# First-group transposes regrouped, chunk loads halved and one weight load moved, at the start of a six-layer cross-network kernel

## The chip, the cores and the metric

The kernel runs on one core of a Trainium2 chip. Times are device microseconds (us). "Time" is a whole execution; "span" is the profiled one, from its first to its last instruction, and is about 1.8 us shorter. PE is the matmul engine (TensorE), DVE is VectorE, ACT is ScalarE; SP is the engine whose queue issues nearly all transfers (DMA).

## The reference

```python
B, F, D, L = 16384, 26, 16, 6        # Din = F*D = 416
x = x0                               # [B, Din] bf16
for l in range(L):
    proj = jnp.einsum('bd,de->be', x, ws[l]) + bs[l]
    x = x0 * proj + x
return x
```

The features number 416 = 3 x 128 + 32. The last 32, the "tails", are handled apart. The kernel keeps the features on the partitions, so x0 must be turned (transposed) on its way in.

## The kernel before

The rows are cut into 8 groups of 2048, a group into 4 chunks of 512. Groups 1 to 7 are turned by the DMA. Group 0 has no time for that: its chunks are loaded as they lie, PE turns them by a matmul with the identity, and ACT and DVE copy the result out of PSUM. The work items are pairs of group and layer, (g, l), in a wavefront order: (0,0), then (1,0), then (0,1), and so on. A pair has three "tiles" of 128 output features, and tails.

Instructions are added one by one with the data that they read and write; a solver derives the semaphore waits. Each engine and each DMA queue keeps the order in which its instructions were added. A transfer on the SP queue that must wait holds up every transfer added after it.

```python
def load_group(g, between=lambda: None):
    ...
    turn(0)                                            # DMA transposes of x0, to SBUF
    add("sp", lambda h: h.dma_start_transpose(Tb, x0[rows, D - P:D]), ...)   # the tails, turned
    turn(1)
    turn(2)
    between()
    for j in range(NJ):                                # four copies: tails to their quadrants
        add("sp", ... h.dma_start(x0s[s][q, XW:XW + CH], Tb[P - T32:P, j * CH:(j + 1) * CH]) ...)
    if turn_of(g, 1):                                  # rotation: waits for the four copies to land
        rotate(x0s[s][:, XW:XW + CH], x0s[s][:, XW + CH:XW + 2 * CH], turn_of(g, 1), ...)
# ... cut: order of the first transfers on SP
load_nat(0, 0, 2)
load_nat(0, 2, KK)
load_wm(0, "sp")                                       # first weights, layer 0
for j in range(1, NJ):
    load_nat(j, 0, KK)                                 # chunks 1 to 3 of group 0
load_w3(0, "sp")
load_group(1, lambda: load_wm(1, "sp"))                # second weights: ahead of the tails' copies
load_wm(2, "sp")
load_w3(2, "sp")

def transposed_chunk(j):
    ba, bb = ((0, 1), (3, 0), (1, 3), (0, 1))[j]       # PSUM banks
    first = (0, P, 2 * P, D - P)                       # 4 x 128 columns: the last holds 32 new ones
    ...                                                # 16 transposes, 2 copies on ACT, 2 on DVE

def first_job():                                       # pair (0, 0)
    transposed_chunk(0)
    ...                                                # bias
    keep_busy(8, 3)                                    # filler matmuls, to hold PE's clock
    full(g, l, 0, ba, True, True, chunks=[0])
    full(g, l, 1, bb, True, True, chunks=[0])
    transposed_chunk(1)
    transposed_chunk(2)
    full(g, l, 0, ba, True, True, chunks=[1])
    transposed_chunk(3)
    load_w3(1, "act")
    full(g, l, 1, bb, True, True, chunks=[1])
    full(g, l, 0, ba, True, True, chunks=[2, 3])
    rows32(g, l, 0, ba, False)                         # the first 32-row matmuls
    ...
```

Of the kernel before, what the change touches and what calls it, by code (L numbers as in the profile page):

```python
# [3 lines left out]
P = 128  # L4
CH = 512
T32 = 32

ACT_F = mybir.ActivationFunctionType
# [13 lines left out]
class Program:  # L22
# [12 lines left out]
    def add(self, eng, fn, reads=(), writes=(), lane=None, batch=None, hold=False, release=False):  # L35
        op = Op(eng, fn, lane, batch)
        deps = {}
        if eng == "pool":
            writes = list(writes) + ["pool"]
        for t in reads:  # L40
            w = self.writer.get(t)
            if w is not None:
                deps[id(w)] = (w, True)
        for t in writes:
            w = self.writer.get(t)
            if w is not None:
                deps[id(w)] = (w, True)
            for r in self.readers.get(t, ()):
                if id(r) not in deps:
                    deps[id(r)] = (r, False)  # L50
        for d, raw in deps.values():
            if d.lane is None and d.eng == eng and lane is None and (eng == "pe" or not raw):
                continue
            op.deps.append(d)
        for t in reads:
            self.readers.setdefault(t, []).append(op)
        for t in writes:
            self.writer[t] = op
            self.readers[t] = []
        if eng == "dve":  # L60
            if hold:
                self.flush()
                self.held = op
            else:
                self.queue[eng].append(op)
                if release:
                    self.flush()
        else:
            self.queue[eng].append(op)
        if lane is not None:  # L70
            batches = self.lanes.setdefault(lane, [])
            if not batches or batches[-1][0] != batch:
                batches.append((batch, []))
            batches[-1][1].append(op)
        return op
# [123 lines left out]
def bass_standalone__cross_network_dcn__recsys_kernel(  # L199
# [6 lines left out]
    B, D = x0.shape  # L206
# [46 lines left out]
    def cols(t, j):  # L253
        return slice(t * GC + j * CH, t * GC + (j + 1) * CH)

    def x0_tok(s, t, j):
        return ("x0", s, t, j)
# [7 lines left out]
    def slot(g):  # L265
        return g % NX0
# [12 lines left out]
    def load_wm(l, eng):  # L279
        add(eng, lambda h: h.dma_start(wm[l][:, :, :], ws[l, 0:NT * P, :].rearrange("(t p) f -> p t f", p=P)),  # L280
            writes=[("wm", l)], lane=f"wm{l}", batch=0)

    def load_w3(l, eng):
        for j in range(NJ):
            add(eng, lambda h, j=j: h.dma_start(w3[l][j * T32:(j + 1) * T32, :], ws[l, NT * P:D, :]),
                writes=[("w3", l, j)], lane=f"w3{l}", batch=0)

    def load_group(g, between=lambda: None):
        s = slot(g)
        rows = slice(g * GC, (g + 1) * GC)  # L290
        def turn(t):
            add("sp", lambda h: h.dma_start_transpose(
                x0s[s][:, t * GC:(t + 1) * GC], x0[rows, t * P:(t + 1) * P]),
                writes=[x0_tok(s, t, j) for j in range(NJ)], lane=f"x0_{s}_{t}", batch=g)

        turn(0)
        add("sp", lambda h: h.dma_start_transpose(Tb, x0[rows, D - P:D]),
            writes=[("ost", t, j) for t in range(NT + 1) for j in range(NJ)], lane="Tb", batch=g)
        turn(1)
        turn(2)  # L300
        between()
        for j in range(NJ):
            q = slice(j * T32, (j + 1) * T32)
            add("sp", lambda h, q=q, j=j: h.dma_start(x0s[s][q, XW:XW + CH], Tb[P - T32:P, j * CH:(j + 1) * CH]),
                reads=[("ost", 0, 0)], writes=[("x03q", s, j)], lane=f"x03_{s}", batch=g)

        if turn_of(g, 1):
            rotate(x0s[s][:, XW:XW + CH], x0s[s][:, XW + CH:XW + 2 * CH], turn_of(g, 1),
                   x03_toks(s), ("x03r", s), f"x03r_{s}", g)

    def x03_toks(s):
        return [("x03q", s, j) for j in range(NJ)]
# [207 lines left out]
    def load_nat(j, k0, k1):  # L520
        add("sp", lambda h: h.dma_start(x0n[:, j, k0:k1, :], perm(g0, j)[:, k0:k1, :]),  # L521
            writes=[("nat", j, k) for k in range(k0, k1)], lane=f"nat{j}{k0}", batch=0)
# [6 lines left out]
    load_nat(0, 2, KK)  # L529
    load_wm(0, "sp")  # L530
    for j in range(1, NJ):
        load_nat(j, 0, KK)
    load_w3(0, "sp")
    load_group(1, lambda: load_wm(1, "sp"))
    load_wm(2, "sp")
    load_w3(2, "sp")

    def keep_busy(n, b):

        for _ in range(n):  # L540
            add("pe", lambda h: h.matmul(bank(b, n=P), ones[:, :], ones[:, :], start=True, stop=True),
                reads=["ones"], writes=[("ps", b)])
# [3 lines left out]
    def psum_t(b):  # L546
        return psum[:, b * CH:(b + 1) * CH].bitcast(BF16)

    def transposed_chunk(j):
        ba, bb = ((0, 1), (3, 0), (1, 3), (0, 1))[j]  # L550
        s = slot(0)
        first = (0, P, 2 * P, D - P)
        seq = [(t, k) for t in range(NT) for k in range(KK)]
        if j == 0:
            seq = [(t, k) for k2 in (0, 2) for t in range(NT) for k in (k2, k2 + 1)]
        for n, (t, k) in enumerate(seq + [(NT, k) for k in range(KK)]):
            if j == 0 and n == NT * 2:
                keep_busy(2, 3)
            b, o = (ba, t * CH) if t < 2 else (bb, (t - 2) * CH)
            c = slice(o + k * P, o + (k + 1) * P)  # L560
            add("pe", lambda h, t=t, k=k, b=b, c=c: h.transpose(  # L561
                psum_t(b)[:, c], x0n[:, j, k, first[t]:first[t] + P], ident[:, :]),
                reads=[("nat", j, k), x0_tok(nat, 0, 0), "ident"], writes=[("ps", b)])
        for t in range(2):
            add("act", lambda h, t=t: h.activation(  # L565
                x0s[s][:, cols(t, j)], psum_t(ba)[:, t * CH:(t + 1) * CH], ACT_F.Copy),
                reads=[("ps", ba)], writes=[x0_tok(s, t, j)])
        add("dve", lambda h: h.tensor_copy(x0s[s][:, cols(2, j)], psum_t(bb)[:, 0:CH]),  # L568
            reads=[("ps", bb)], writes=[x0_tok(s, 2, j)])
        q = slice(j * T32, (j + 1) * T32)  # L570
        add("dve", lambda h: h.tensor_copy(x0s[s][q, XW:XW + CH], psum_t(bb)[P - T32:P, CH:2 * CH]),
            reads=[("ps", bb)], writes=[("x03q", s, j)])

    def first_job():

        g, l = 0, 0
        start_job(g, l)
        transposed_chunk(0)
        bt = 7
        for t in range(NT):  # L580
            add("pe", lambda h, t=t: h.transpose(
                psum_t(bt)[:, t * 8:t * 8 + L], brow[0:L, t * P:(t + 1) * P], ident[0:L, 0:L]),
                reads=["brow", "ident"], writes=[("ps", bt)])
        for j in range(NJ):
            q = slice(j * T32, (j + 1) * T32)
            add("pe", lambda h, j=j, q=q: h.matmul(
                psum_t(bt)[q, NT * 8:NT * 8 + L], brow[0:L, NT * P:D], ident[0:L, 0:L],
                is_transpose=True, tile_position=(0, j * T32)),
                reads=["brow", "ident"], writes=[("ps", bt)])
        add("act", lambda h: h.activation(  # L590
            bias[:, :, :], psum_t(bt)[:, 0:32].rearrange("p (t l) -> p t l", l=8)[:, :, 0:L], ACT_F.Copy),
            reads=[("ps", bt)], writes=["bias"])
        keep_busy(8, 3)
        ba, bb = [4, 5, 6, 7], [2, 3, 0, 1]
        full(g, l, 0, ba, True, True, chunks=[0])
        full(g, l, 1, bb, True, True, chunks=[0])
        transposed_chunk(1)
        transposed_chunk(2)
        full(g, l, 0, ba, True, True, chunks=[1])
        transposed_chunk(3)  # L600
        load_w3(1, "act")
        full(g, l, 1, bb, True, True, chunks=[1])
        full(g, l, 0, ba, True, True, chunks=[2, 3])
        rows32(g, l, 0, ba, False)
        evacuate(g, l, 0, ba, [0, 1], 2, vector=[2, 3])
        full(g, l, 1, bb, True, True, chunks=[2, 3])
        rows32(g, l, 1, bb, False)
        rows32(g, l, 2, ba, True)
        evacuate(g, l, 1, bb, list(range(NJ)), 2)
        full(g, l, 2, ba, False, True, lambda j: evacuate(g, l, 2, ba, [j], 1))  # L610
        finish_tile(g, l, NT)
        tails([(g, l)])
# [341 lines left out]
```

## Time and profile before

| | before |
|---|---|
| time, median of 3 runs | 476.69 us (476.66 to 477.77) |
| span of the profiled run | 475.7 us |
| PE busy | 462.2 us, 97% |
| PE's share of the chain of waits | 95% |

The page of the kernel before: busy time by engine, then the chain that ended last, by engine.

```profile
PE 462.2 (97%) x3325; PEld 195.7 (41%) x3379; DVE 404.0 (85%) x696; ACT 342.4 (72%) x372; POOL 6.8 (1%) x15
...
PE 95%; issue 1%; DMA 1%; ACT 1%; DVE 1%; SPq 0%
```

PE is the limit nearly everywhere. The timeline of PE (columns: start, length, engine, line, operation, count; in brackets the idle time before and what ended it) shows where the start is not dense.

```profile
4.01 0.72 PE L561 MATMUL ps<-ident,x 128*128 128x128 bf16 x10
...
5.81 1.24 PE L456 MATMUL ps<-x,wm 128*128 128x512 bf16 x5 [0.25 <-ACT x L565]
7.92 1.07 PE L561 MATMUL ps<-ident,x 128*128 128x128 bf16 x16 [0.87 <-DMA x<-in_x_dram]
9.56 1.05 PE L561 MATMUL ps<-ident,x 128*128 128x128 bf16 x16 [0.57 <-DVE x L568]
10.45 0.81 PE L456 MATMUL ps<-x,wm 128*128 128x512 bf16 x3
11.10 1.06 PE L561 MATMUL ps<-ident,x 128*128 128x128 bf16 x16
12.21 1.89 PE L456 MATMUL ps<-x,wm 128*128 128x512 bf16 x8
14.03 0.40 PE L477 MATMUL ps<-x,w 32*128 32x512 bf16 x4
...
22.78 0.61 PE L477 MATMUL ps<-x,w 32*128 32x512 bf16 x8
23.32 5.35 PE L456 MATMUL ps<-x,wm 128*128 128x512 bf16 x24
28.60 0.43 PE L471 MATMUL ps<-x,w 32*32 32x512 bf16 x16
```

L561 are the transposes, L456 the 128-row matmuls, L477 the 32-row ones. At 7.92 and 9.56 us PE resumes after waiting for the second and the third chunk. (The view names a DVE copy at 9.56; the landing records show that chunk complete at 9.42.) From there it has no wait. The piece at 23.32 us holds 24 matmuls: the second tile of pair (1,0), then, from the 13th matmul at 25.92 us on, the first tile of pair (0,1). That is the first user of the second weights.

The SP queue in the same stretch (here the length is the time that the queue spent on the issue).

```profile
13.60 4.38 SPq L292 DMA_TRANSPOSE x<-in_x_dram  x2
18.02 0.59 SPq L280 DMA_DIRECT2D wm<-in_ws_dram  x1
18.66 2.52 SPq L304 DMA_DIRECT2D x<-ost  x4
22.55 0.53 SPq L325 DMA_DIRECT2D x<-x  x1
23.12 0.60 SPq L326 DMA_DIRECT2D x<-x  x1
23.76 0.58 SPq L280 DMA_DIRECT2D wm<-in_ws_dram  x1
```

The second weights (L280 at 18.02) landed at 21.82 us, 4 us before their use. L304 are the four copies of the tails; L325 and L326, the rotation, sit waiting from 21.2 to 22.55 us for those copies to land; only then can the third weights (L280 at 23.76) be issued. They landed at 26.90 us, 3.1 us later.

### The profile page before, as it was taken

To read this page: it belongs to the slowest core of one execution; us is meant where nothing else is said; L and a number is where in the kernel's file an instruction comes from. 1 tells how busy PE (TensorE), PEld (TensorE's weight loads), DVE (VectorE), ACT (ScalarE), POOL (GpSimd) and SP (SyncE) were. 2 spreads that over 40 slices of the span, in tenths; PEclk is the share of its full clock that TensorE was granted. 3 is DMA by queue.
4 is the path that set the end of the run, shared out by engine and by line. 5 is a ranking of instruction groups with operands and counts; after the bars stand their busy time and mean duration, and the time that the engine had idled before them with its cause. 6 is when DMAs were issued, how large, how long until landed. Compare 5 with 4: busy or idle time off the path is not lost.

```text
span 475.7 us, 8355 instructions
## 1 busy us (share of the span) xinstructions
PE 462.2 (97%) x3325; PEld 195.7 (41%) x3379; DVE 404.0 (85%) x696; ACT 342.4 (72%) x372; POOL 6.8 (1%) x15
## 2 busy tenths in 40 slices
PE   7999999999999999999999999999999999999995
PEld 6344444444444444444444444434444444444442
DVE  2888888888888888898889869988888888888896
ACT  4677777777777777777777777777777777777785
POOL 1000000000000000000000000000000000000000
PEclk9999999999999999999999999999999999999999
DMA  8866950640002397369308940990000039025899
GB/s 223 181 150 137 190 113 1 142 81 1 28 7 44 63 228 158 76 139 244 84 21 195 208 108 9 178 279 2 1 10 25 4 64 242 15 45 117 227 155 288
DMA packets 138363, 53.31 MB, mean 112 GB/s; under 512 B 112330, under 2 KB 137428, under 8 KB 138324
## 3 DMA queue, kind: packets, MB, share of 16 engines
q1 hardware_dynamic: 137848, 52.46, 49.2%
q8 instruction: 26, 0.43, 0.4%
q10 hardware_dynamic: 476, 0.32, 0.2%
q14 instruction: 13, 0.11, 0.1%
HBM read 5.97 MB, written 13.63 MB: 41 GB/s over the span
## 4 chain that ended last, share of the span: by engine, by line
PE 95%; issue 1%; DMA 1%; ACT 1%; DVE 1%; SPq 0%
PE ps L456 77%; PE ps L477 7%; PE ps L497 6%; PE ps L798 2%; DMA x<-in_x_dram 1%; PE ps L471 1%; ACT tw L394 1%; PE ps L561 1%; PE ps L488 1%; DVE x L864 0%; PE ps L809 0%; ACT x L852 0%; DVE x L858 0%; PE ps L841 0%; SPq L521 0%
## 5 line engine op out<-in xcount | busy, mean ns | idle before, releaser
L394 ACT ACTIVATE tw<-ps,bias 128x1024 bf16<-128x1024 f32 (+1 forms) x295 | 299.8, 1071 | 119.8 <-PE ps L477 80.7
L456 PE MATMUL ps<-x,wm 128*128 128x512 bf16 x1638 | 371.7, 379 | 5.8 <-issue 3.7
L456 PEld LDWEIGHTS ps<-x,wm 128*128 128x128 bf16 x1692 | 158.9, 98 | 213.5 <-issue 27.9
L403 DVE TENSOR_TENSOR tw<-tw,x 128x1024 bf16<-128x1024 bf16 (+1 forms) x285 | 192.3, 682 | 52.8 <-ACT tw L394 52.4
L408 DVE TENSOR_TENSOR x<-tw,x 128x1024 bf16<-128x1024 bf16 (+1 forms) x285 | 183.0, 682 | 0.0
L477 PE MATMUL ps<-x,w 32*128 32x512 bf16 x512 | 39.2, 379 | 0.0
L497 PE MATMUL ps<-x,wm 128*32 128x512 bf16 x564 | 33.0, 380 | 0.0
L434 ACT ACTIVATE ts<-ps,bias 128x512 bf16<-128x512 f32 x47 | 28.8, 701 | 0.0
L438 DVE TENSOR_TENSOR x<-ts,x 128x512 bf16<-128x512 bf16 x47 | 18.6, 417 | 3.7 <-DMA x<-x 3.6
L497 PEld LDWEIGHTS ps<-x,wm 128*32 128x32 bf16 x564 | 13.8, 96 | 17.6 <-issue 5.3
L477 PEld LDWEIGHTS ps<-x,w 32*128 32x128 bf16 x512 | 7.8, 92 | 27.6 <-issue 27.1
L436 DVE TENSOR_TENSOR ts<-ts,x 128x512 bf16<-128x512 bf16 x47 | 18.5, 417 | 0.0
L666 POOL COPY ost<-ot 128x512 bf16<-128x512 bf16 x6 | 5.4, 898 | 423.7 <-DMA ot<-x 423.7
L798 PE MATMUL ps<-wm,x 128*128 128x416 bf16 x48 | 9.5, 340 | 0.0
L852 ACT ACTIVATE x<-ps 128x416 bf16<-128x416 f32 x16 | 7.7, 533 | 2.0 <-PE ps L798 1.9
L568 DVE COPY x<-ps 128x512 bf16<-128x512 bf16 x4 | 1.7, 424 | 8.7 <-PE ps L561 8.7
L565 ACT ACTIVATE x<-ps 128x512 bf16<-128x512 bf16 x8 | 4.3, 594 | 5.6 <-PE ps L561 5.6
L798 PEld LDWEIGHTS ps<-wm,x 128*128 128x128 bf16 x48 | 4.3, 98 | 4.2 <-issue 1.0
L561 PE MATMUL ps<-ident,x 128*128 128x128 bf16 x64 | 4.6, 226 | 1.4 <-DMA x<-in_x_dram 0.9
L858 DVE TENSOR_TENSOR x<-x,x 128x832 bf16<-128x832 bf16 (+1 forms) x10 | 5.0, 504 | 1.1 <-ACT x L852 1.1
L488 PE MATMUL ps<-x,w 32*32 32x512 bf16 x188 | 5.9, 374 | 0.0
L471 PE MATMUL ps<-x,w 32*32 32x512 bf16 x208 | 5.6, 385 | 0.0
(38 smaller groups left out, 35.7 us busy)
## 6 DMA issues: line engine op xcount, KB each, us to landing
out_dram<-ost SPq DMA_DIRECT2D x6, 1664.0 KB, 7.1
x<-in_x_dram SPq DMA_DIRECT2D x7, 416.0 KB, 8.0
x<-x SPq DMA_DIRECT2D x24, 96.0 KB, 2.2
wm<-in_ws_dram SPq DMA_DIRECT2D x6, 312.0 KB, 3.7
out_dram<-ost SPq DMA_DIRECT2D x2, 832.0 KB, 6.7
x<-x SPq DMA_DIRECT2D x22, 64.0 KB, 2.0
out_dram<-x SPq DMA_DIRECT2D x3, 416.0 KB, 3.6
x<-ost SPq DMA_DIRECT2D x28, 32.0 KB, 2.2
```

What stands on the lines that cost most here:

```text
L394: add("act", lambda h, a=a, w=w, b0=b0: h.activation(tw[r][:, a * CH:(a + w) * CH], psum[:, b0 * CH:(b0 + w) * CH], ACT_F.Identity, bias=b ...
L403: add("dve", lambda h, a=a, e=e: h.tensor_tensor(tw[r][:, a * CH:e * CH], tw[r][:, a * CH:e * CH], x0s[s0][:, i * GC + a * CH:i * GC + e * ...
L408: add("dve", lambda h, a=a, e=e: h.tensor_tensor(xs[so][:, i * GC + a * CH:i * GC + e * CH], tw[r][:, a * CH:e * CH], src(i, a, e), ALU.ad ...
L434: add("act", lambda h: h.activation(ts[r][:, :], bank(b), ACT_F.Identity, bias=bias[:, 3, l:l + 1], scale=1.0), reads=[("ps", b), "bias"], ...
L436: add("dve", lambda h: h.tensor_tensor(ts[r][:, :], ts[r][:, :], x03, ALU.mult), reads=[("ts", r)] + tok0, writes=[("ts", r)], release=True)
L438: add("dve", lambda h: h.tensor_tensor(x3s[so][:, :], ts[r][:, :], res, ALU.add), reads=[("ts", r)] + rtok, writes=[("x3", so), ("x3", so, ...
L456: add("pe", lambda h, t=t, j=j: h.matmul(bank(banks[j]), wm[l][:, t, ecols], src(t, j, j + 1), start=(first and t == 0), stop=(not first a ...
L471: add("pe", lambda h, q=q, j=j, r=r, c=c, o=o: h.matmul(psum[o, banks[j] * CH:(banks[j] + 1) * CH], w3[l][q, i * P + c * T32:i * P + (c + ...
L477: add("pe", lambda h, q=q, j=j, r=r: h.matmul(bank(banks[j]), w3[l][q, ecols], src[q, :], start=first, stop=not first, tile_position=(r * ...
L488: add("pe", lambda h, l=l, b=b, s3=s3, ri=ri, qi=qi, ro=ro, qo=qo: h.matmul(psum[qo, b * CH:(b + 1) * CH], w3[l][qi, NT * P:D], s3[qi, :], ...
L497: add("pe", lambda h, t=t, j=j, src=src, l=l, b=b, ro=ro, qo=qo: h.matmul(psum[qo, b * CH:(b + 1) * CH], wm[l][:, t, NT * P:D], src(t, j, ...
L798: add("pe", lambda h, t=t: h.matmul(bank(b, n=D), xcol(t, j, kk), wm[l][:, t, :], start=(first and t == 0), stop=(not first and t == NT - 1)),
```

## The change

The intent, as I read it from the edit: fewer transposes (the tails of all four chunks at once on the four column tiles of the array, in place of a fourth 128-column transpose for each chunk), less waiting for loads and banks, and tails of group 1 that come earlier, since PE is to need them earlier.

```diff
-        load_nat(j, 0, KK)
+        load_nat(j, 0, 2)
+        load_nat(j, 2, KK)
...
-    load_group(1, lambda: load_wm(1, "sp"))
+    load_group(1)
+    load_wm(1, "sp")
...
 def transposed_chunk(j):
-        ba, bb = ((0, 1), (3, 0), (1, 3), (0, 1))[j]
+        ba, bb = ((0, 1), (3, 0), (6, 7), (0, 1))[j]
...  # 12 transposes, first row half then second; copies: 2 on ACT, 1 on DVE
+    def transposed_tails(b):
+        for k in range(KK):
+            for j in range(NJ):
+                o = slice(j * T32, (j + 1) * T32)
+                add("pe", lambda h, j=j, k=k, o=o: h.matmul(
+                    psum_t(b)[o, k * P:(k + 1) * P], x0n[:, j, k, NT * P:D], ident[:, :],
+                    is_transpose=True, tile_position=(0, j * T32)), ...)
+        add("dve", lambda h: h.tensor_copy(x0s[s][:, XW:XW + CH], psum_t(b)[:, 0:CH]), ...)
...
-        keep_busy(8, 3)
+        keep_busy(5, 3)
...
         full(g, l, 0, ba, True, True, chunks=[1])
+        full(g, l, 1, bb, True, True, chunks=[1])
         transposed_chunk(3)
+        transposed_tails(7)
         load_w3(1, "act")
-        full(g, l, 1, bb, True, True, chunks=[1])
         full(g, l, 0, ba, True, True, chunks=[2, 3])
```

## The prediction

> **What bounds the kernel now.** The page gives TensorE (PE) 462.2 us busy of a 475.7 us span (97%); the chain of waits is 95% PE. From about 12 us on that chain is matmuls and short "issue" steps, with no wait for a transfer. So only the first 26 us, which the change touches, can move the time, and each us won or lost there reaches the end.
>
> The start is gated by the loads of the first group. In the chain the second chunk's load ends at 7.88 us; its 16 transposes take 1.08 us; the third chunk's start at 9.56. The waits view blames a VectorE copy for that gap; the landings show the third chunk at about 9.4, so I read it as the load. Both come late from one of 16 DMA engines, 1.4 to 1.9 us behind the others. From 9.56 to 14.10 PE is full: 32 transposes and 12 matmuls.
>
> **What the change does.**
> 1. Transposes: 64 full ones (about 65 ns each in the timeline) become 48, plus 16 tail transposes on four column tiles. After 9.5 us PE has 18 full ones left instead of 32: about -0.9 us. The tails cost about 0.5 us, an estimate: the Trainium skill, "TensorE: Matmul & The Clock Gate" (Wait — 56ns, not 53.3ns?), gives a floor of about 25 ns start to start, and "TensorEngine Tiling (Array Packing)" (Key Properties) says that a switch of tiling mode drains the array. In this trace 12 column-tile matmuls of 512 columns take 0.76 us, so tiles do overlap; no run yet shows the short ones.
> 2. Halved loads: the first half is turned while the second flies; the second halves land no earlier. Three more issues of about 0.48 us go on the SP queue, mostly hidden, since it is held up there (an input transpose issue takes 4.1 us against about 2.1 later).
> 3. VectorE makes one tail copy of 0.43 us instead of four; own banks remove possible bank waits. Fewer filler matmuls: nothing.
> Sum on PE by 14 us: -0.3 us (0 to -0.6).
> 4. The second weights move behind the next group's tails and their rotation. Before, they were issued at 18.02 and landed at 21.8; PE needs them at 25.97. After, the tails go out 0.6 us earlier and land near 21.8; the rotation copies wait for that and take 1.2 us; the weights are issued at about 23.1. The third weights landed 3.1 us after issue, so these land at 26.2 to 26.8. PE would arrive at about 25.6: a new PE wait of 0.5 to 1.2 us, which swallows the gain.
>
> **Net.** PE enters that tile at about 26.3 instead of 25.97: +0.3 us. Predicted 477.0 us against 476.69, 8 in 10 within 475.6 to 478.4. Faster by over 2%: 0.5%; within 2%: 99%; slower: 0.5%.
>
> **What would show it.** (a) Chunk transposes in bursts of 6, the first before 7.9 us. (b) One burst of 16 tails of about 0.5 us near 12.5 us. (c) Chunks two and three of tile 0 done near 13.8. (d) A PE wait for the second weights' transfer near 25.6 us, up to 1.2 us: the decisive one. (e) From there on the same time to the end.
>
> **What would make it wrong.** The weights land under 3 us from issue: the gain of about 0.3 us survives. The extra issues are not hidden and shift the next group's transposes by up to 1.4 us: the wait grows to 2 us and more. The slow DMA engine is a chance of this run. Column-tile transposes dearer than 60 ns each would eat step 1. The three runs before spread over 1.1 us, more than the effect.

## The result

| | before | changed |
|---|---|---|
| time, median of 6 runs | 477.32 us (476.66 to 477.77) | 477.90 us (477.53 to 479.31) |
| ratio | | 1.0018, 95% interval 1.0003 to 1.0033 |
| span of the profiled run | 475.7 us | 476.2 us |

A ratio is the mean time of one kernel's fast runs over that of the other's fast runs of the same rounds, so it is not quite the ratio of the medians. The change made the kernel longer by a hair, within 2%. The page of the changed kernel:

```profile
PE 468.3 (98%) x3376; PEld 195.3 (41%) x3376; DVE 402.6 (85%) x693; ACT 342.0 (72%) x372; POOL 6.2 (1%) x15
...
PE 93%; SPq 4%; DVE 1%; ACT 1%; DMA 0%; issue 0%
```

The PE busy times do not compare: of the matmuls of before 54 have no record (3325, beside 3379 weight loads), of the changed kernel none. By the weight loads, PE does three matmuls fewer (3376), the three fillers. The new item is SPq, the SP queue, with 4% of the chain. PE's timeline of the changed kernel (L559 transposes, L579 the tail transposes, L455 128-row matmuls, L476 32-row ones, L470 the marker):

```profile
4.16 0.85 PE L559 MATMUL ps<-ident,x 128*128 128x128 bf16 x6
...
5.82 1.45 PE L455 MATMUL ps<-x,wm 128*128 128x512 bf16 x6
7.11 1.50 PE L559 MATMUL ps<-ident,x 128*128 128x128 bf16 x24
8.52 1.74 PE L455 MATMUL ps<-x,wm 128*128 128x512 bf16 x6
10.10 0.83 PE L559 MATMUL ps<-ident,x 128*128 128x128 bf16 x12
10.87 0.41 PE L579 MATMUL ps<-ident,x 128*32 128x128 bf16 x16
11.21 1.50 PE L455 MATMUL ps<-x,wm 128*128 128x512 bf16 x6
12.64 0.40 PE L476 MATMUL ps<-x,w 32*128 32x512 bf16 x4
...
21.83 0.61 PE L476 MATMUL ps<-x,w 32*128 32x512 bf16 x8 [0.16 <-DMA x<-ost]
22.37 2.76 PE L455 MATMUL ps<-x,wm 128*128 128x512 bf16 x12
26.43 2.75 PE L455 MATMUL ps<-x,wm 128*128 128x512 bf16 x12 [1.29 <-DVE x L407]
29.11 0.43 PE L470 MATMUL ps<-x,w 32*32 32x512 bf16 x16
```

PE reached the first 32-row matmuls at 12.64 us instead of 14.03. Nine us later it waits 0.16 us for the tails, and then it stands still from 25.14 to 26.43 us. The marker, which comes right after the first user of the second weights, is at 29.11 us instead of 28.60: 0.5 us late, as the span is. So 1.4 us were won and 1.9 us lost. (From start to start the two stops cost 0.22 and 1.45 us, as the idle time in brackets begins only where the last matmul's end is modelled; the other 0.2 us went at the eight 32-row matmuls near 14.4 us, which took 0.76 us to the next start, before 0.54.) The SP queue of the changed kernel:

```profile
12.78 5.15 SPq L292 DMA_TRANSPOSE x<-in_x_dram  x2
17.97 2.51 SPq L303 DMA_DIRECT2D x<-ost  x4
21.80 0.53 SPq L324 DMA_DIRECT2D x<-x  x1
22.38 0.60 SPq L325 DMA_DIRECT2D x<-x  x1
23.02 1.12 SPq L280 DMA_DIRECT2D wm<-in_ws_dram  x2
```

L324 and L325, the rotation, had to wait until 21.80 us for the tails' copies, and the second weights (the first of the two L280 at 23.02) come after it. Their last piece landed at 26.29 us, and PE goes on at 26.43. The waits view of the changed kernel, between 20 and 30 us, names other causes, DVE for the matmul and ACT for its weight load (columns: who, for whom, total, times, longest):

```profile
PEld ps L455 <- ACT tw L393: 1.8, 1, 1.8
PE ps L455 <- DVE x L407: 1.3, 1, 1.3
PEld ps L476 <- DMA x<-ost: 0.6, 1, 0.6
```

DVE's addition (L407) did end at 26.31 us by its timeline, but by the program it makes output of pair (1,0), which this tile of pair (0,1) does not read. The view takes the release that came last by its records, so the name alone decides nothing. The experiments have to.

### The profile page after: what moved, and what is told of

It is laid out like the page before. It is cut to its first block, busy times and chain, and to the rows that moved or that the text cites. A ratio compares the mean times of both kernels' runs of the same rounds, so it can differ in the third digit from the quotient of the medians.

```text
span 476.2 us, 8401 instructions
## 1 busy us (share of the span) xinstructions
PE 468.3 (98%) x3376; PEld 195.3 (41%) x3376; DVE 402.6 (85%) x693; ACT 342.0 (72%) x372; POOL 6.2 (1%) x15
## 4 chain that ended last, share of the span: by engine, by line
PE 93%; SPq 4%; DVE 1%; ACT 1%; DMA 0%; issue 0%
PE ps L455 76%; PE ps L476 7%; PE ps L496 7%; PE ps L811 2%; SPq L292 2%; PE ps L470 1%; SPq L520 1%; SPq L297 1%; PE ps L487 1%; ACT tw L393 0%; DMA x<-ost 0%; SPq L303 0%; SPq L285 0%; DVE x L877 0%; DVE x L407 0%
## 5 line engine op out<-in xcount | busy, mean ns | idle before, releaser
L455 PE MATMUL ps<-x,wm 128*128 128x512 bf16 x1692 | 379.8, 380 | 1.4 <-DVE x L407 1.3
L455 PEld LDWEIGHTS ps<-x,wm 128*128 128x128 bf16 x1692 | 158.6, 98 | 215.5 <-issue 28.2
L407 DVE TENSOR_TENSOR x<-tw,x 128x1024 bf16<-128x1024 bf16 (+1 forms) x285 | 182.9, 682 | 0.0
L476 PE MATMUL ps<-x,w 32*128 32x512 bf16 x512 | 39.4, 379 | 0.2 <-DMA x<-ost 0.2
L496 PEld LDWEIGHTS ps<-x,wm 128*32 128x32 bf16 x564 | 13.8, 96 | 17.6 <-issue 5.3
L476 PEld LDWEIGHTS ps<-x,w 32*128 32x128 bf16 x512 | 7.8, 92 | 28.1 <-issue 27.1
L470 PE MATMUL ps<-x,w 32*32 32x512 bf16 x208 | 5.6, 385 | 0.0
L877 DVE TENSOR_TENSOR x<-x,x 128x832 bf16<-128x832 bf16 x8 | 4.6, 586 | 0.4 <-DMA x<-x 0.4
```

The costliest lines, as they stand in the source:

```text
L407: add("dve", lambda h, a=a, e=e: h.tensor_tensor(xs[so][:, i * GC + a * CH:i * GC + e * CH], tw[r][:, a * CH:e * CH], src(i, a, e), ALU.ad ...
L455: add("pe", lambda h, t=t, j=j: h.matmul(bank(banks[j]), wm[l][:, t, ecols], src(t, j, j + 1), start=(first and t == 0), stop=(not first a ...
L470: add("pe", lambda h, q=q, j=j, r=r, c=c, o=o: h.matmul(psum[o, banks[j] * CH:(banks[j] + 1) * CH], w3[l][q, i * P + c * T32:i * P + (c + ...
L476: add("pe", lambda h, q=q, j=j, r=r: h.matmul(bank(banks[j]), w3[l][q, ecols], src[q, :], start=first, stop=not first, tile_position=(r * ...
L496: add("pe", lambda h, t=t, j=j, src=src, l=l, b=b, ro=ro, qo=qo: h.matmul(psum[qo, b * CH:(b + 1) * CH], wm[l][:, t, NT * P:D], src(t, j, ...
```

## The experiments

Eleven kernels were run, in three sets. Each was timed in 5 rounds beside the kernel before, whose medians in the three sets were 477.16, 477.20 and 477.30 us (wm_later has 4 timed runs, before_fill5 has 6). "Marker" is the start of the first 32-by-32 matmuls in the one profiled execution.

| run | second weights issued | transposes, loads | median us | ratio to before (95%) | marker us | span us |
|---|---|---|---|---|---|---|
| before | ahead of the tails | old, whole | 477.32 | 1 | 28.60 | 475.7 |
| changed | behind the rotation | new, halves | 477.90 | 1.0018 (1.0003 to 1.0033) | 29.11 | 476.2 |
| before_again | ahead of the tails | old, whole | 477.07 | 0.9997 (0.9985 to 1.0010) | 28.15 | 475.3 |
| after_again | behind the rotation | new, halves | 478.56 | 1.0026 (1.0013 to 1.0040) | 29.61 | 476.7 |
| wm_back | ahead of the tails | new, halves | 477.52 | 1.0006 (0.9992 to 1.0019) | 27.89 | 475.0 |
| wm_mid | between tails and rotation | new, halves | 476.53 | 0.9988 (0.9975 to 1.0000) | 27.84 | 474.9 |
| wm_late_only | behind the rotation | old, whole | 477.68 | 1.0011 (0.9997 to 1.0025) | 28.57 | 475.7 |
| wm_later | behind the third weights | new, halves | 482.09 | 1.0113 (1.0095 to 1.0130) | 32.82 | 480.1 |
| before_wm_mid | between tails and rotation | old, whole | 476.70 | 0.9994 (0.9980 to 1.0007) | 27.77 | 474.8 |
| mid_old_turns | between tails and rotation | old, halves | 477.27 | 1.0004 (0.9992 to 1.0017) | 28.28 | 475.4 |
| mid_whole_loads | between tails and rotation | new, whole | 476.34 | 0.9987 (0.9975 to 1.0000) | 27.62 | 474.7 |
| before_fill5 | ahead of the tails | old, whole, 5 fillers | 477.23 | 1.0003 (0.9989 to 1.0018) | 28.08 | 475.2 |
| best_fill8 | between tails and rotation | new, whole, 8 fillers | 476.44 | 0.9985 (0.9973 to 0.9997) | 28.33 | 475.4 |

One profile of a kernel is one draw. The first loads land at different times in each. The clock differs too: by the traces' clock records it was granted in full from 3.84 and 5.84 us on in the two profiles of the kernel before, from 5.57 and 7.03 us in the two of the changed kernel (in before the 128-column matmuls start 107 ns apart ahead of that point and 56 ns after it). Markers of one and the same kernel differ by 0.45 us (28.60 and 28.15) and 0.5 us (29.11 and 29.61). Waits inside a profile are therefore better evidence than marker against marker.

**before_again and after_again: how fixed is what the profiles show?** The edit is a comment.

> The kernel before with only a comment added: it shows the spread and whether the late DMA engine (landings of the second and third chunk 1.4 to 1.9 us behind the other 15 engines) is fixed or chance. If it is fixed, the second chunk's transposes start again near 7.9 us and the tile that first uses the second weights near 26.0. If it is chance, they start near 7.1 us, and that tile starts up to 0.8 us earlier than 26.0. Ratio 1.000 within 0.0015.

> The changed kernel with only a comment added, beside the kernel before on the same chip: the wait before the first tile of the second weights comes back within 0.3 us of 1.29 if it is fixed by the issue order; the rival, a chance of the first profile, gives a wait under 0.5 us or none. Ratio to before 1.0005 to 1.0025.

In before_again the second chunk landed at 7.24 us, its last engine 0.14 us behind the one before it (1.37 us in the first profile). Its transposes began at 7.59 us, without a wait, and the marker came at 28.15. So the late DMA engine of the first profile was chance. In after_again the wait came back, with the second weights complete at 26.80 us:

```profile
26.93 2.75 PE L455 MATMUL ps<-x,wm 128*128 128x512 bf16 x12 [1.25 <-DVE x L407]
```

That it comes back is what a cause in the order of the transfers predicts; the next runs test that.

**wm_back, wm_mid: is the wait for the second weights?** Against the changed kernel:

```diff
 # wm_back, in load_group, ahead of the tails' copies:
+        between()
-    load_group(1)
-    load_wm(1, "sp")
+    load_group(1, between=lambda: load_wm(1, "sp"))
 # wm_mid, in load_group, behind the tails' copies, ahead of the rotation:
+        after_tails()
-    load_group(1)
-    load_wm(1, "sp")
+    load_group(1, after_tails=lambda: load_wm(1, "sp"))
```

> The change with the second weights put back ahead of the next group's tails. My theory (the new 1.29 us wait of PE at 25.1 us is for the second weights): this wait is gone, the tails land about 0.65 us later, PE waits about 0.8 us for them at the first 32-row matmuls near 22 us, the first tile of the second weights starts near 25.75 us, and the time is about 0.7 us under the change as it stands. Rival (the wait is for the VectorE addition that the view names): a wait of over 1 us stays at that place, with VectorE ending its addition 0.1 us before PE goes on.

PE's timeline of wm_back (lines numbered as in the kernel before):

```profile
22.06 0.61 PE L477 MATMUL ps<-x,w 32*128 32x512 bf16 x8 [0.39 <-DMA x<-ost]
22.60 5.35 PE L456 MATMUL ps<-x,wm 128*128 128x512 bf16 x24
27.89 0.43 PE L471 MATMUL ps<-x,w 32*32 32x512 bf16 x16
```

The long wait is gone: the 24 matmuls from 22.60 us run through. In its place PE waits 0.39 us for the tails (I expected about 0.8), which land 0.23 us later than in the changed kernel (I expected 0.65). Its median (477.52) is 0.4 us under the changed kernel's, in other rounds; that difference the intervals do not resolve, and the profile, not the time, carries the verdict.

> The change with the second weights between the next group's tails and their rotation: they need not wait for the tails to land. My theory: issued near 20.5 us, landed by 24 us, no PE wait at 25.1 us, only the 0.16 us for the tails stays; time 1.3 us under the change as it stands, 0.3 to 0.8 us under the kernel before (ratio 0.9983 to 0.9994). Rival (VectorE addition): the wait stays and the time is that of the change.

PE and then the SP queue of wm_mid:

```profile
22.02 0.61 PE L477 MATMUL ps<-x,w 32*128 32x512 bf16 x8
22.56 5.35 PE L456 MATMUL ps<-x,wm 128*128 128x512 bf16 x24
27.84 0.43 PE L471 MATMUL ps<-x,w 32*32 32x512 bf16 x16
```

```profile
17.84 2.52 SPq L303 DMA_DIRECT2D x<-ost  x4
20.39 0.59 SPq L280 DMA_DIRECT2D wm<-in_ws_dram  x1
21.66 0.53 SPq L325 DMA_DIRECT2D x<-x  x1
```

The weights (L280 at 20.39) are issued in the time that the queue otherwise spends waiting for the tails, and land at 23.64 us. Both waits are gone. DVE's additions stand in the same order as in the changed kernel and end at 26.49 us, 1.3 us after PE began the tile (25.16 us), so the rival falls. ACT falls with it: its work stands in the same order too, and the waits view has at most 0.4 us of PE's weight loads for it, where the changed kernel had 1.8. The ratio of 0.9988 was expected between 0.9983 and 0.9994.

**wm_late_only: the move alone.** The kernel before with `load_group(1)` and then `load_wm(1, "sp")`.

> The kernel before with only the move of the second weights. My theory: it brings only the loss. PE reaches the first tile of the second weights near 25.6 to 26.0 us and the weights land near 26.2: a wait of 0.3 to 0.9 us that the kernel before has not, time 0.3 to 0.9 us longer than before (ratio 1.0006 to 1.002). Rival (the move costs nothing; the loss comes from the transposes or halves): ratio 1.000, no wait.

The weights landed at 25.76 us, and PE waited 0.16 us for them; the view names the transfer:

```profile
25.89 2.75 PE L456 MATMUL ps<-x,wm 128*128 128x512 bf16 x12 [0.16 <-DMA wm<-in_ws_dram]
```

The size is under my 0.3 to 0.9 us. A later PE is not enough to explain it: PE came at 25.73 us, in after_again at 25.68, and there it waited 1.25 us. What differs is the landing, 25.76 against 26.80 us, because the tails ahead of it were issued at 17.48 against 18.52 us (17.97 in the first profile of the changed kernel). The halved loads put three more issues on this queue, so they may be part of that; the rest is scatter, and no run separates the two. Ratio 1.0011, interval from 0.9997: a small loss or none.

**wm_later: the dose.** The changed kernel with the second weights behind the third.

```diff
     load_group(1)
-    load_wm(1, "sp")
     load_wm(2, "sp")
     load_w3(2, "sp")
+    load_wm(1, "sp")
```

> The change with the second weights one place later still, behind the third weights. The wait is for the transfer if it grows with it: issue near 25.4 us, landing near 28.6, PE wait 3.5 us instead of 1.29, time about 2.3 us over the change (ratio to before 1.005 to 1.008). Rival (VectorE addition, or a noise of the start): wait stays near 1.3 us, time as the change.

PE's timeline and the stretches of wm_later (columns of the latter: length, busy us and count by engine, then the granted PE clock, DMA share, GB/s):

```profile
22.39 2.76 PE L455 MATMUL ps<-x,wm 128*128 128x512 bf16 x12
28.69 4.20 PE L455 MATMUL ps<-x,wm 128*128 128x512 bf16 x12 [3.53 <-DMA wm<-in_ws_dram]
32.82 0.60 PE L470 MATMUL ps<-x,w 32*32 32x512 bf16 x16
```

```profile
25.00:28.60 3.60, 0.15 (x1) 0.00 (x0) 3.40 (x7) 2.10 (x3) 0.00 (x0) 1.00 0.81 232
28.60:33.00 4.40, 4.31 (x28) 1.54 (x36) 0.42 (x1) 0.00 (x0) 0.00 (x0) 0.64 1.00 140
```

The weights landed at 28.55 us and PE waited 3.53 us, as expected from the issue order, and here the view names the weights' transfer. But the time grew by 4.2 us over the changed kernel (482.09 against 477.90, in other rounds), not by 2.3. The rest is in the second fence: after the long stop the granted clock was 0.64 on average until 33 us (by the clock records full until 29.82 us, then half until 33.23), and the 12 matmuls took 4.20 us instead of 2.75. That agrees with the Trainium skill, "TensorE: Matmul & The Clock Gate" (Part 1), which says that the clock is halved after an idle window of about 3.4 us. The clock fell only 1.1 us after PE had gone on, though. The 1.29 us of the changed kernel stay under it: its clock from 25.0 to 28.6 us was 1.00.

**before_wm_mid, mid_old_turns, mid_whole_loads: what are the other parts worth?** All with the second weights between tails and rotation. The first is the kernel before with that alone; mid_old_turns adds the halved loads; mid_whole_loads is wm_mid with whole loads, so the new transposes without the halves.

> The kernel before with only the second weights put between the next group's tails and their rotation, nothing else. If that place is only harmless, there is no PE wait before (as in the kernel before, where the weights came 4 us early) and none after: ratio 1.000 within 0.001, the first tile of the second weights starts as in the kernel before, 25.4 to 26.0 us. Rival (that place is itself the gain of the best version, by bringing the tails earlier): time 0.6 us under before, ratio 0.9988.

> The same and the halved loads, with the old transposes (tails turned in each chunk, banks shared). If the halves alone bring the gain, ratio about 0.9988; if they need the new order of transposes, as I think since the old order needs all four row groups of a chunk after four transposes, ratio 1.000 to 1.001.

> The best version so far (second weights between tails and rotation) with whole chunk loads instead of halves: new transposes alone. My theory: the saving is in the number of transposes and in the banks, not in the halves, as PE was busy until 7.1 to 7.7 us in runs where the chunk lands at 7.2: time within 0.3 us of that version (ratio to before 0.998 to 0.9995), last column-tile transpose near 11.3 to 12.0 us. Rival (the halves carry the gain): time as before, ratio 1.000.

The place alone is harmless (0.9994; its interval, 0.9980 to 1.0007, holds both 1 and the rival's 0.9988, so a gain from the place is not ruled out). The tile of the second weights began at 25.09 us there, ahead of my 25.4 to 26.0. The halves brought no gain where they could be seen: with the old transposes 1.0004 with them and 0.9994 without, and the new transposes run at 0.9987 without them and at 0.9988 with them. The new transposes show in the profiles, as the time from the second chunk's first transpose to the first 32-row matmuls: 5.82 us in each of before_again, wm_late_only, before_wm_mid, mid_old_turns and before_fill5; 5.52 us in each of the changed kernel, wm_back, wm_later, mid_whole_loads and after_again. That is 0.30 us. So the new transposes are worth 0.30 us in the profiles; by time alone they are not told from the old ones with the same place (0.9987 and 0.9994, intervals overlapping). (The five old ones each include a wait of 0.21 to 0.28 us at the third chunk, for a bank or for its load. Left out are before, wm_mid and best_fill8, which waited 0.57, 0.24 and 0.37 us for the third chunk's load; they took 6.10, 5.58 and 5.73.)

**before_fill5, best_fill8: the fillers.** `keep_busy(8, 3)` against `keep_busy(5, 3)`, in the kernel before and in mid_whole_loads.

> The kernel before with five filler matmuls instead of eight after the first chunk. My prediction counted this as nothing. In two profiles of the old transposes the first real matmul started 0.35 and 0.68 us after the first weights had landed, in all of the new ones 0.13 us. If the fillers are that gap, it becomes 0.13 to 0.2 us and the first tile starts up to 0.5 us earlier when the weights land early: ratio 0.9990 to 1.000. If not (the four tail transposes of the first chunk, or chance), the gap stays.

> The best version (new transposes, whole loads, second weights between tails and rotation) with eight fillers again. If the three fillers cost, first real matmul 0.2 to 0.5 us after the first weights landed instead of 0.13, and a ratio to before of 0.999; if they cost nothing, 0.9987 as without them.

In before_fill5 the first real matmul started 0.14 us after the first weights had landed (5.69 us). The 0.35 us on which I rested the question (in before, and in before_again too) was a misreading: a matmul is missing from the records. In before the weight loads of these six matmuls (the timeline of PE's weight loads) begin at 5.57 us, and PE's timeline above has five matmuls from 5.81:

```profile
5.57 0.99 PEld L456 LDWEIGHTS ps<-x,wm 128*128 128x128 bf16 x6 [0.18 <-ACT x L565]
```

With the missing matmul put 0.215 us (the distance of its neighbours) ahead of the first recorded one, both have 0.14 us, as before_wm_mid, mid_old_turns and best_fill8 have, all with eight fillers. Only wm_late_only, corrected likewise, has more, 0.47 us: there the clock was half until 6.53 us, and the eighth filler started at 6.46, after the weights' landing at 6.09. So the fillers cost about 0.3 us in one profile of the six with eight of them, and neither ratio shows it. before_fill5 measured 1.0003 (expected 0.9990 to 1.000); best_fill8 was expected at 0.999 or at 0.9987 and measured 0.9985.

## Why the prediction was right

The time (477.0 us predicted, 477.90 measured, range 475.6 to 478.4) and the mechanism held (as a difference, +0.3 us was forecast; the ratio of 1.0018 is +0.9 us, with an interval of 0.1 to 1.6): the start gets shorter, and the second weights, now behind a waiting transfer, give it all back. Point by point:

- **(d) A wait for the second weights near 25.6 us, up to 1.2 us.** It came at 25.14 us and lasted 1.29, and in the second profile at 25.68 us and lasted 1.25. The landing was predicted at 26.2 to 26.8 us and fell at 26.29 and 26.80. Moving the load removed the wait, moving it further grew it to 3.53 us. This is shown.
- **The sum on PE, -0.3 us.** The runs give 0.30 us, but not by the terms that I added, so that the sum agrees is in part luck. The 16 tails took 0.34 us to the next instruction, not 0.5. I had taken the 25 ns from start to start of "TensorE: Matmul & The Clock Gate"; in the trace the four column tiles start 3 to 4 ns apart and each round of four follows the last by 55 to 66 ns, so four tails cost about one full transpose (56 ns from start to start in the run of 24; I had counted 65). Over the stretch from the second chunk on, 12 full transposes fewer (0.67 us) and the tails give -0.33 us. The bank wait, which I called "possible", was real: before_again waited 0.28 us at the third chunk for ACT's copy out of the shared bank. Without it the gain should be about 0.6 us. What took that back is likely a new wait inside the matmul groups: the six matmuls after the transposes take 1.58 us (8.52 to 10.10), where six need about 1.3, and the waits view of the changed kernel between 6 and 13 us charges PE's weight loads (PEld) with 0.7 us for ACT's copies:

```profile
PEld ps L455 <- ACT x L571: 0.7, 2, 0.4
```

  That is read from one view, not tested.
- **(c) Tile 0 done near 13.8 us.** It was done at 12.64. The step that failed is the starting point: I took 7.88 and 9.56 us, set by one late DMA engine, as the base of both kernels. I had named that lateness as a possible chance, and before_again shows that it was one. That the time came out all the same is no merit of the sum: an earlier PE only waits longer for the weights.
- **(a) Transposes in bursts of six.** Wrong: 24 ran in a row from 7.11 us, since the loads were there. For the same reason the halves brought nothing measurable. **(b)** One burst of 16 tails: yes, 0.41 us long by its records, near 10.9 us.
- **(e) The same time from there on.** From the marker to the end: 447.1 us in both.
- **"Fewer filler matmuls: nothing."** Right in time, within what 5 rounds resolve; one profile of six shows about 0.3 us.
- **The three extra issues** were mostly hidden, as predicted: the transfer after the last input transpose was issued at 18.05 us on average in the six profiles with halves (17.46 to 18.52) and at 17.62 in the seven with whole loads (17.39 to 18.03), so about 0.43 us of 3 x 0.48 came through, in ranges that overlap. This delays the tails and the weights behind them too.

So the step that was off is a term of the sum, the start: its work was sized right at 0.3 us, its base was one slow draw.

What stays open: how the gain of 0.6 to 0.7 us in the best versions (ratio 0.9985 to 0.9988) splits between fewer transposes, own banks, the tails' earlier copies and the place of the second weights. mid_whole_loads is about 0.3% under the changed kernel (0.9987 over 1.0018, from different rounds) and 0.1% under the kernel before, with an interval that ends at 1.0000; best_fill8's ends at 0.9997.

## What to carry to other kernels

An in-order queue of transfers has a place where it stands still for another transfer to land; here a load put behind that place paid the whole wait, and put just ahead of it cost nothing that the times show. When the stage before gets faster, check the landing time of every later load against its new time of use, not only of the load that was late last time. And profile a kernel twice before a late transfer in one profile is taken as the base of a sum. Before a short gap is read as a wait, count the matmuls against their weight loads: one missing record looked like 0.2 us here.

## What the Trainium skill lacked or had wrong

- "TensorE: Matmul & The Clock Gate": its floor of about 25 ns from start to start is not the cost of short matmuls on column tiles. Here four transposes of 128 columns started 3 to 4 ns apart, and 16 took 0.34 us, 21 ns each. The page's own section on small matmuls (Part 3) says that tiles start about 4 ns apart; the two statements stand apart.
- "DMA: Bandwidth & Descriptors" names two engines as usually slower, and ties that to software-made descriptors (SWDGE); the loads here went by SP's queue, which the page of the profile lists as hardware_dynamic. One engine of 16 was 1.4 to 1.9 us behind at the second and third chunk in the first profile of the kernel before, 0.8 and 0.7 us at the second chunk in wm_late_only's and best_fill8's, and 0.1 us in the second profile of the kernel before. The trace does not name the engine. No page says how much landings scatter from run to run; here the first weights landed between 5.46 and 6.46 us.
- "TensorE: Matmul & The Clock Gate" does not say how idle a window must be for the clock to fall. Here, in wm_later, PE stood for 3.53 us until 28.69 us; the half clock began at 29.82 us and lasted 3.41 us. The changes of the clock in this trace lie 7, 1 and 131 times 3.413 us apart. If a window of that length ended at 29.82 us, PE was at work in the last 1.1 us of it.
